# The attention of a fused attention and feed-forward kernel, beside the second product, recast as quadrants of 64 by 64

## The chip, the cores and the metric

The kernel runs on one core of one Trainium2 chip. The metric is the device time of one execution in microseconds (us). TensorE (PE in the profile, its weight loads PEld) multiplies into PSUM; VectorE (DVE), ScalarE (ACT) and GpSimd (POOL) do the rest; SyncE (SP) issues most of the transfers.

## The reference, cut to what matters

```
q_n = q / sqrt(mean(q*q) + 1e-6) * g_q            # k likewise; batch 8, heads 12, seq 448, head_dim 64
attn = softmax((q_n @ k_n.T) / sqrt(64))          # per batch and head, 448 x 448
x = (attn @ v) laid out as (8*448, 12*64)         # 3584 x 768
h = x @ w_in                                      # 768 -> 2048
out = (max(h, 0) ** 2) @ w_out                    # 2048 -> 768
```

All arrays are f32 on the chip.

## The kernel before, in words

The unit of the attention is a *pair*: two heads of one batch entry, 64 dimensions each, so that both fill 128 partitions. There are 8 * 6 = 48 pairs. The feed-forward part works on *spans* of two batch entries, four spans in all. Both products of a span are done by a scheme with seven products of blocks instead of eight (the names A11, S1, S2 and so on); the sums that this scheme needs are made by VectorE and GpSimd.

The order of every engine's work is written out by hand (a manual schedule): each engine executes in the order in which the Python code issues. The program runs as follows.

1. `attention_alone` does the 12 pairs of the first span (i below NAT = 12) while the weights are prepared.
2. For each span: `first_product` (matmuls on L1042), then `second_product` (matmuls into `ps`, L1089). Beside the second product of spans 0, 1 and 2 runs `attention` for the 12 pairs of the next span: both are generators, and the loop takes a share of the second product's matmuls after each `yield` of the attention. The last span's second product runs alone.

The change touches only the 36 pairs of `attention`, thus three stages. One iteration i of it issues, in this order:

- `scores(i, 0)` and `scores(i, 1)` (matmuls L758): keys in chunks of 128 (NF = 3 whole chunks, c = 0 to 2, and a rest of 64 keys, c = 3), all 448 queries as the moving operand. The result has keys on partitions; head h goes to its own PSUM bank, `sc[:, h]`. ScalarE turns both heads of a chunk into `pr` with one Exp (L761). The tiles of `sc` come from a pool of two, so chunks 3 and 2 wait for the Exp of chunks 0 and 1; `pr` goes to one of five places that are used in turn, one of which `fold` of the pair before has just read (L793).
- `values(i - 1)`, which calls `later_values`: the value product of the pair before. Head h fills partitions h*64 to h*64+63 of the bank `pav` (L834). The rest of 64 keys is laid out on 128 partitions as two halves of 224 queries (`sides`), in the tile `half`; its second half goes to another bank, `rest` (L840).
- `spread(i - 1)`: two DMAs on ScalarE's queue (L805) that copy the pair's softmax factors to the partitions of `xT`. They wait for the factors' way through DRAM (L992, on SP's queue).
- `scores(i, 3)` and `scores(i, 2)`, then ScalarE's copy of `rest` out of PSUM (L968), then `norm_by_squares` and `transposes` for later pairs.
- VectorE adds up the exponentials (`add_up`, L782 and L784), does `finish(i - 1)` (L876 adds `rest` to `pav`, L877 multiplies by the factors and writes `xT`), and `fold(i)` (L792 to L799), which makes the factors.

In an iteration's schedule the second product's matmuls come between these steps, mostly after the last scores. Its results leave PSUM through VectorE (L1100 to L1108) or ScalarE (L1098) and are written out by `deliver` (L1077, L1080). In span 0, VectorE makes the second product's sums as well (`combine`, L1003 to L1007).

A matmul of this kernel shows as two records of TensorE, each with its own weight load. The form `64*128` in the profile means 64 rows of contraction and 128 columns of weights; `64*64` is a quadrant of the array.

Of the kernel before, what the change touches and what calls it, by code (L numbers as in the profile page):

```python
# [9 lines left out]
F32 = mybir.dt.float32  # L10
U32 = mybir.dt.uint32
AF = mybir.ActivationFunctionType
ALU = mybir.AluOpType
# [373 lines left out]
def attention_then_ffn_bounded(  # L387
# [35 lines left out]
    nc = tc.nc  # L423

    B, H, S, D = q.shape
    NT, DM = out.shape
    DFF = w_in.shape[1]
    P = 128
# [9 lines left out]
    NF = S // P  # L438
    sides = [slice(m * P // 2, (m + 1) * P // 2) for m in range(2)]
# [15 lines left out]
    ps_o = ctx.enter_context(tc.tile_pool(name="ps_o", bufs=1, space=bass.MemoryType.PSUM))  # L455
# [8 lines left out]
    qk, qkT, ident, mhalf, gains, rstd0, _ = held  # L464
# [189 lines left out]
    vs, probs, pavs, tots, normed, rstds = {}, {}, {}, {}, {}, {0: rstd0}  # L654
    places, halves, rests = [], [], {}
    sums = {"out": [dram.tile([2 * S // 32, 32], F32, name=f"factors{n}") for n in range(2)]}

    def load(i):
        if i < NAT:
            load_q(nc, qk, q, i)  # L660
            load_k(nc, qk, k, i)
            return

        b, h0 = i // NPAIR, 2 * (i % NPAIR)
        for s, src in enumerate((q, k)):
            dst = by_squares(i, 0)[:, s]
            for n in range(4):
                nc.sync.dma_start(dst[n * 32:(n + 1) * 32],
                                  src[b, h0 + n // 2, :, n % 2 * 32:n % 2 * 32 + 32]
                                  .rearrange("(g t) e -> t g e", t=32))  # L670
# [38 lines left out]
    def squares(i):  # L709
        raw, qkn = (by_squares(i, n).rearrange("p s g e -> p (s g e)") for n in range(2))  # L710
        nc.scalar.activation(qkn, raw, AF.Square)
# [19 lines left out]
    def transposes(i):  # L731

        qkn = normed.pop(i)
        for s in range(2):
            nc.vector.transpose(qkT[:, 0, s], qkn[:, s].rearrange("p g e -> p (g e)"))
        nc.scalar.activation(qkT[:, 0, 0], qkT[:, 0, 0], AF.Copy, scale=gains[:, 0:1])
# [11 lines left out]
    def scores(i, c):  # L748


        if i >= NAT:
            sc = ps_s.tile([P, 2, 512], F32, tag="s", name="sc")
            n = S if c < NF else S // 2
            for h in range(2):
                rows = slice(h * D, (h + 1) * D)
                for m in range(S // n):
                    part = slice(0, P) if c < NF else sides[m]
                    nc.tensor.matmul(sc[part, h, 0:n], qkT[rows, 0, 1, c * P:min((c + 1) * P, S)],  # L758
                                     qkT[rows, 0, 0, m * n:(m + 1) * n], start=True, stop=True)
            pr = probs[i, c] = places[(NF * i + c) % len(places)] if c < NF else halves[i % 2]  # L760
            nc.scalar.activation(pr, sc[:, :, 0:n], AF.Exp)  # L761
            return
        at = i % 2
        sc = ps_s.tile([SP, 2, 512], F32, tag="s", name="sc")
        for h in range(2):
            rows = slice(h * D, (h + 1) * D)
            nc.tensor.matmul(sc[:, h, 0:S], qkT[rows, at, 1, c * SP:(c + 1) * SP], qkT[rows, at, 0, :],  # L767
                             start=True, stop=True)
        pr = probs[i, c] = places[(NJ * i + c) % len(places)][:SP]
        for h in range(2):  # L770
            nc.scalar.activation(pr[:, h], sc[:, h, 0:S], AF.Exp, scale=rstds[i][:, 1, 2 * c + h:2 * c + h + 1])
# [4 lines left out]
    def add_up(i, c):  # L776

        acc = acc_of(i)
        if i >= NAT and c == NF:
            for m, rows in enumerate(sides):  # L780
                part = acc[rows, :, m * S // 2:(m + 1) * S // 2]
                nc.vector.tensor_tensor(part, part, probs[i, c][rows], ALU.add)  # L782
            return
        nc.vector.tensor_tensor(acc, probs[i, 0] if c == 1 else acc, probs[i, c], ALU.add)  # L784
# [16 lines left out]
    def spread(i):  # L801

        b, hp = divmod(i, NPAIR)
        for h in range(2):
            nc.scalar.dma_start(xT[h * D:(h + 1) * D, b % 2, hp],  # L805
                                sums["out"][i % 2].rearrange("(h g) t -> h () (g t)", h=2)[h].to_broadcast([D, S]))
# [12 lines left out]
    def values(i, chunks=range(NJ)):  # L819
        if 0 in chunks:  # L820
            pavs[i] = ps_o.tile([P, S], F32, tag="o", name="pav") if i >= NAT or i % 2 == 0 else bank("pav", 1)
        if i >= NAT:
            return later_values(i)
        for c in chunks:
            for h in range(2):
                nc.tensor.matmul(pavs[i][h * D:(h + 1) * D, :], vs[i][:SP, h, c, :], probs[i, c][:, h, :],  # L826
                                 start=(c == 0), stop=(c == NJ - 1))

    def later_values(i):


        for c in range(NF):
            for h in range(2):
                nc.tensor.matmul(pavs[i][h * D:(h + 1) * D, :], vs[i][:, h, c, :], probs[i, c][:, h, :],  # L834
                                 start=(c == 0), stop=False)
        rests[i] = ps_o.tile([P, S], F32, tag="t", name="rest")
        for h in range(2):
            for m, rows in enumerate(sides):
                into = rests[i] if m else pavs[i]
                nc.tensor.matmul(into[h * D:(h + 1) * D, 0:S // 2], vs[i][rows, h, NF, :], probs[i, NF][rows, h, :],  # L840
                                 start=bool(m), stop=True)

    def added(i):

# [12 lines left out]
    def finish(i):  # L857

        b, hp = divmod(i, NPAIR)
        pav, factors = pavs.pop(i), xT[:, b % 2, hp]  # L860
        x = factors
        if i < NAT:


            turned, factors = sums["turned"], sums["factors"]
            few = small.tile([P, S // 32], F32, tag="few", name="few", bufs=1)
            nc.vector.transpose(turned, tots.pop(i))
            nc.vector.reciprocal(few, turned.rearrange("p (g r) -> p g r", r=32)[:, :, 0])
            nc.vector.transpose(factors.rearrange("p (g r) -> p g r", r=32),
                                few.rearrange("p g -> p g ()").to_broadcast([P, S // 32, 32]))  # L870

            x = x.rearrange("d (p j) -> d j p", j=NJ)
            pav, factors = (t.rearrange("d (j p) -> d j p", j=NJ) for t in (pav, factors))
        else:
            half = pav[:, S // 2:]
            nc.vector.tensor_tensor(half, half, rests.pop(i), ALU.add)  # L876
        nc.vector.tensor_tensor(x, pav, factors, ALU.mult)  # L877
        del vs[i]

# [14 lines left out]
    def attention_alone():  # L894


        for i in range(NAT):
# [34 lines left out]
            total_of(i - 1)  # L932
            values(i, (0, 1))
            finish(i - 1)
            yield
            if added(i) == 3:
# [5 lines left out]
        values(i, (2, 3))  # L942
        total_of(i)
        finish(i)
        combine_x(i)

    def attention(first):


        last = first + 2 * NPAIR  # L950
        for i in range(first, last + 1):
            if i < last:
                scores(i, 0)
                scores(i, 1)
            if i + 3 < min(last + 2, B * NPAIR):
                load(i + 3)
            if i == first:
                yield
            if i > first:
                values(i - 1)  # L960
                spread(i - 1)
            if i < last:
                add_up(i, 1)
                scores(i, 3)
                scores(i, 2)
            if i > first:
                rest = halves[(i - 1) % 2].rearrange("p h q -> p (h q)")[:, 0:S // 2]
                nc.scalar.copy(rest, rests[i - 1][:, 0:S // 2])  # L968
                rests[i - 1] = rest
            if i + 2 < last:  # L970
                norm_by_squares(i + 2)
            yield
            if i + 1 < last:
                transposes(i + 1)
            if i < min(last, B * NPAIR - 1):
                load_v(i + 1)
            yield
            if i < last:
                add_up(i, 2)
                add_up(i, 3)  # L980
            if i > first:
                finish(i - 1)
            if i + 3 < last:
                squares(i + 3)
            yield
            if i < last:
                fold(i)
            if i > first:
                combine_x(i - 1)
            yield  # L990
            if i < last:
                nc.sync.dma_start(sums["out"][i % 2], sums["square"][0:2 * S // 32, 1])  # L992
            yield
# [168 lines left out]
    for span in range(NSPAN):  # L1162
# [7 lines left out]
        with tc.tile_pool(name="second_product", bufs=2, reuse_waits="tile") as work:  # L1170
            rest = second_product(work, span)
# [101 lines left out]
```

## Time and profile before

| | |
|---|---|
| three runs | 1391.18, 1392.67 (median), 1393.52 us |
| profiled execution, first to last instruction (span) | 1389.0 us; the median lies 3.7 us above it, and no other time of the profiled execution is given |
| TensorE busy | 1360.9 us, 98% of the span |
| VectorE, GpSimd, ScalarE busy | 60%, 41%, 30% |
| `attention` beside the second product | about 263 to 457, 600 to 787 and 930 to 1115 us |
| scores L758, forms 64\*128 and 64\*64 | 432 and 288 records |
| values L834 (128\*64), rests L840 (64\*64) | 432 and 288 records |
| L876, L877 (VectorE), L968 (ScalarE) | 36 each, 400, 624 and 346 ns |

How to read it: an engine that is busy 98% of the span sets the time nearly everywhere, and the others matter where TensorE waits for them. A record of a matmul overlaps the next, so what one costs is the distance between starts, not its duration.

### The profile page before, as it was taken

The page shows a single profiled execution, that of the slowest core. Times are in us where ns is not written, and L with a number is a line of the kernel's source. Part 1 is how long each engine was busy: PE and PEld are TensorE (multiplying, and loading weights), DVE is VectorE, ACT ScalarE, POOL GpSimd, SP SyncE. Part 2 cuts the span into 40 slices and gives each one's busy share as a digit, 9 for nine tenths or more (in the row PEclk, how much of TensorE's full clock was granted, in tenths as well). Part 3 has the DMA queues.
Part 4 walks back from the last instruction along what each step waited for, and adds up shares of the span by engine and source line. Part 5 has one row for each costly group of instructions (what it writes and reads, how often), then busy time and mean ns, then how long its engine had stood idle before and what let it go on. Part 6 is the DMA issues. An engine that isn't in the chain of part 4 may idle for free.

```text
span 1389.0 us, 15124 instructions
## 1 busy us (share of the span) xinstructions
PE 1360.9 (98%) x4738; PEld 636.1 (46%) x4738; DVE 829.7 (60%) x1470; ACT 418.0 (30%) x657; POOL 572.1 (41%) x397
## 2 busy tenths in 40 slices
PE   8989999999999999999999999999999999999997
PEld 3333455444444455444444455444444445554553
DVE  6889676599987333477877623457888723332111
ACT  7875555422332011233332111233333201110000
POOL 5998878544343022644344122445445302220000
PEclk9999999999999999999999999999999999999999
DMA  8687998544666333344665432345574442333443
GB/s 239 194 231 197 327 387 307 160 107 106 125 134 130 102 87 86 99 116 105 134 144 120 106 99 86 100 104 116 109 148 108 103 103 85 88 91 100 109 112 67
DMA packets 436678, 190.02 MB, mean 137 GB/s; under 512 B 283244, under 2 KB 434540, under 8 KB 436588
## 3 DMA queue, kind: packets, MB, share of 16 engines
q1 hardware_dynamic: 426988, 180.23, 50.2%
q10 hardware_dynamic: 9472, 8.72, 2.4%
q8 instruction: 40, 0.66, 0.2%
q14 instruction: 50, 0.41, 0.1%
q0 software_dynamic: 128, 0.00, 0.0%
HBM read 155.72 MB, written 33.16 MB: 136 GB/s over the span
## 4 chain that ended last, share of the span: by engine, by line
PE 85%; DVE 6%; POOL 3%; issue 2%; DMA 2%; ACT 2%; SPq 1%; ACTq 0%; POOLq 0%
PE ps L1089 33%; PE pd L1042 10%; PE pa L1042 10%; PE pc L1042 10%; PE sc L758 7%; PE pav L834 5%; PE pb L1042 5%; PE sc L767 1%; PE pav L840 1%; PE tot L854 1%; PE pav L826 1%; POOL rstd L702 1%; DMA sw<-w1s 1%; POOL gC L566 1%; DMA factors<-square 1%
## 5 line engine op out<-in xcount | busy, mean ns | idle before, releaser
L1089 PE MATMUL ps<-gT,sw 128*128 128x448 f32 x768 | 299.2, 543 | 0.8 <-POOL gT L1019 0.8
L724 POOL TENSOR_TENSOR half<-half,mhalf 128x28 f32<-128x28 f32 x36 | 173.6, 4822 | 267.6 <-DVE half L723 249.3
L1089 PE MATMUL ps<-gC,sw 128*128 128x448 f32 x576 | 225.5, 543 | 2.9 <-ACT p L1098 1.5
L1019 POOL TENSOR_TENSOR gT<-gT 128x448 f32<-128x448 f32 x96 | 94.9, 990 | 303.7 <-ACT gT L1015 303.7
L1089 PEld LDWEIGHTS ps<-gT,sw 128*128 128x128 f32 x768 | 144.1, 190 | 149.3 <-issue 145.2
L1089 PEld LDWEIGHTS ps<-gC,sw 128*128 128x128 f32 x576 | 107.9, 190 | 115.8 <-issue 108.4
L1042 PE MATMUL pa<-xT,sw 128*128 128x448 f32 x384 | 154.9, 540 | 0.0
L1015 ACT ACTIVATE gT<-gT 128x448 f32<-128x448 f32 x96 | 55.4, 577 | 311.1 <-DVE gT L1057 311.1
L758 PE MATMUL sc<-qkT 64*128 64x448 f32 (+1 forms) x720 | 118.8, 484 | 0.7 <-ACT pr L761 0.4
L761 ACT ACTIVATE pr<-sc 128x896 f32<-128x896 f32 x87 | 77.3, 914 | 133.1 <-DVE quarters L793 62.1
L1042 PEld LDWEIGHTS pa<-xT,sw 128*128 128x128 f32 x384 | 73.0, 190 | 71.6 <-issue 70.5
L1057 DVE TENSOR_TENSOR gT<-z,pd 128x448 f32<-128x448 f32 x32 | 19.8, 620 | 99.7 <-PE pd L1042 99.7
L1042 PE MATMUL pb<-xC,sw 128*128 128x448 f32 x192 | 77.5, 540 | 1.5 <-issue 1.5
L1042 PE MATMUL pc<-xC,sw 128*128 128x448 f32 x192 | 77.5, 540 | 0.6 <-DMA sw<-w1s 0.6
L1042 PE MATMUL pd<-xT,sw 128*128 128x448 f32 x192 | 77.9, 542 | 0.0
L1042 PE MATMUL pd<-xC,sw 128*128 128x448 f32 x192 | 77.5, 540 | 0.1
L1042 PE MATMUL pc<-xT,sw 128*128 128x448 f32 x192 | 77.4, 539 | 0.0
L834 PE MATMUL pav<-pr,vt 128*64 128x448 f32 x348 | 74.2, 548 | 3.2 <-DVE xT L877 3.2
L726 POOL TENSOR_TENSOR qk<-qk,half 128x448 f32<-128x448 f32 x72 | 74.2, 1051 | 2.8
L572 POOL TENSOR_TENSOR gC<-gC 128x384 f32<-128x384 f32 x64 | 73.2, 1161 | 2.5
L758 PEld LDWEIGHTS sc<-qkT 64*128 64x128 f32 (+1 forms) x720 | 46.2, 165 | 54.3 <-issue 42.9
L1049 DVE TENSOR_TENSOR z<-p,pb 128x448 f32<-128x448 f32 x32 | 19.8, 619 | 82.4 <-PE pb L1042 82.4
(132 smaller groups left out, 1757.0 us busy)
## 6 DMA issues: line engine op xcount, KB each, us to landing
sw<-w1s SPq DMA_DIRECT2D x224, 192.0 KB, 2.4
sw<-w2s SPq DMA_DIRECT2D x168, 256.0 KB, 3.3
w1s<-gC SPq DMA_DIRECT2D x8, 1344.0 KB, 7.6
w2s<-gC SPq DMA_DIRECT2D x8, 1344.0 KB, 8.7
out_dram<-osb SPq DMA_DIRECT2D x184, 56.0 KB, 1.9
qk<-in_q_dram SPq DMA_DIRECT2D x144, 56.0 KB, 2.9
qk<-in_k_dram SPq DMA_DIRECT2D x144, 56.0 KB, 2.6
xT<-factors ACTq DMA_DIRECT2D x72, 112.0 KB, 3.4
```

The costliest lines, as they stand in the source:

```text
L572: nc.gpsimd.tensor_tensor(*[blocks_of(n)[:, i] for i in (dst, x, y)], op)
L724: nc.gpsimd.tensor_tensor(half, half, mhalf, ALU.pow)
L726: nc.gpsimd.tensor_tensor(qkn[:, s], raw[:, s], half[:, s * NG:(s + 1) * NG].rearrange("p g -> p g ()").to_broadcast([P, NG, 32]), ALU.mult)
L758: nc.tensor.matmul(sc[part, h, 0:n], qkT[rows, 0, 1, c * P:min((c + 1) * P, S)], qkT[rows, 0, 0, m * n:(m + 1) * n], start=True, stop=True)
L761: nc.scalar.activation(pr, sc[:, :, 0:n], AF.Exp)
L834: nc.tensor.matmul(pavs[i][h * D:(h + 1) * D, :], vs[i][:, h, c, :], probs[i, c][:, h, :], start=(c == 0), stop=False)
L1015: nc.scalar.activation(g, src, AF.Relu)
L1019: nc.gpsimd.tensor_tensor(g, g, g, ALU.mult)
L1042: nc.tensor.matmul(ps, stream[n + i][:, c], rhs[:, c], start=first and c == 0, stop=c == HC - 1, skip_group_check=not first)
L1049: add(z, p1, ps, ALU.add)
L1057: add(g, x, ps, ALU.add)
L1089: nc.tensor.matmul(ps, stream[n][:, c % 4], rhs_of[i][:, c], start=c == 0, stop=c == HF - 1)
```

## The change

All scores of `attention` are issued as quadrants: a chunk of 128 keys becomes two matmuls of 64 keys per head, on the two halves of the output partitions. All value products are issued as quadrants too: a chunk of 128 keys is split into its two halves of partitions, the first accumulating in `pav` and the second in `rest`, both over the full 448 queries. Scores go from 10 to 16 matmuls per pair, values from 10 to 16. Because `rest` now holds a partial sum for all 448 queries, ScalarE copies 448 columns of it where it copied 224, VectorE adds 448 columns where it added 224, and writes the sum to SBUF (into the copy of `rest`), from which the multiplication then reads. The order of all steps, the tiles and their numbers are as before.

```diff
@@ scores
-                for m in range(S // n):
-                    part = slice(0, P) if c < NF else sides[m]
-                    nc.tensor.matmul(sc[part, h, 0:n], qkT[rows, 0, 1, c * P:min((c + 1) * P, S)],
-                                     qkT[rows, 0, 0, m * n:(m + 1) * n], start=True, stop=True)
+                for m, part in enumerate(sides):
+                    keys = slice(c * P + m * D, c * P + (m + 1) * D) if c < NF else slice(NF * P, S)
+                    of = slice(0, S) if c < NF else slice(m * n, (m + 1) * n)
+                    nc.tensor.matmul(sc[part, h, 0:n], qkT[rows, 0, 1, keys], qkT[rows, 0, 0, of], start=True, stop=True)
@@ later_values
-        for c in range(NF):
+        rests[i] = ps_o.tile([P, S], F32, tag="t", name="rest")
+        for c in range(NF + 1):
             for h in range(2):
-                nc.tensor.matmul(pavs[i][h * D:(h + 1) * D, :], vs[i][:, h, c, :], probs[i, c][:, h, :],
-                                 start=(c == 0), stop=False)
-        rests[i] = ps_o.tile([P, S], F32, tag="t", name="rest")
-        for h in range(2):
-            for m, rows in enumerate(sides):
-                into = rests[i] if m else pavs[i]
-                nc.tensor.matmul(into[h * D:(h + 1) * D, 0:S // 2], vs[i][rows, h, NF, :], probs[i, NF][rows, h, :],
-                                 start=bool(m), stop=True)
+                for m, rows in enumerate(sides):
+                    into = (rests[i] if m else pavs[i])[h * D:(h + 1) * D]
+                    into = into if c < NF else into[:, m * S // 2:(m + 1) * S // 2]
+                    nc.tensor.matmul(into, vs[i][rows, h, c, :], probs[i, c][rows, h, :],
+                                     start=(c == 0), stop=(c == NF), skip_group_check=True)
@@ finish
-            half = pav[:, S // 2:]
-            nc.vector.tensor_tensor(half, half, rests.pop(i), ALU.add)
+            rest = rests.pop(i)
+            nc.vector.tensor_tensor(rest, pav, rest, ALU.add)
+            pav = rest
         nc.vector.tensor_tensor(x, pav, factors, ALU.mult)
@@ attention
-                rest = halves[(i - 1) % 2].rearrange("p h q -> p (h q)")[:, 0:S // 2]
-                nc.scalar.copy(rest, rests[i - 1][:, 0:S // 2])
+                rest = halves[(i - 1) % 2].rearrange("p h q -> p (h q)")
+                nc.scalar.copy(rest, rests[i - 1])
```

## The prediction

> **What bounds the kernel now.** I read the page's busy shares first, then the chain of waits, then the timeline of TensorE within one iteration of the attention, then the windows of its stages.
>
> ```profile
> span 1389.0 us, 15124 instructions
> PE 1360.9 (98%) x4738; PEld 636.1 (46%) x4738; DVE 829.7 (60%) x1470; ACT 418.0 (30%) x657; POOL 572.1 (41%) x397
> ...
> PE 85%; DVE 6%; POOL 3%; issue 2%; DMA 2%; ACT 2%; SPq 1%; ACTq 0%; POOLq 0%
> ```
>
> TensorE sets the time nearly everywhere. But its busy time hides gaps between tiling forms; these show in the starts. One iteration (start, length, records):
>
> ```profile
> 408.61 1.78 PE L758 MATMUL sc<-qkT 64*128 64x448 f32 x8
> 410.32 2.48 PE L834 MATMUL pav<-pr,vt 128*64 128x448 f32 x12
> 412.72 0.40 PE L840 MATMUL pav<-half,vt 64*64 64x224 f32 x1
> ...
> 412.96 0.35 PE L840 MATMUL pav<-half,vt 64*64 64x224 f32 x1
> ...
> 413.15 1.51 PE L758 MATMUL sc<-qkT 64*64 64x224 f32 x12
> 414.59 4.78 PE L1089 MATMUL ps<-gC,sw 128*128 128x448 f32 x12
> ```
>
> The x12 at 413.15 holds 8 records of 64\*64 and 4 of 64\*128. The unit comes from the weight loads of the second product, one per record:
>
> ```profile
> 410.31 0.20 PEld L834 LDWEIGHTS pav<-pr,vt 128*64 128x64 f32 x4 [0.65 <-DVE quarters L795]
> 410.75 0.14 PEld L834 LDWEIGHTS pav<-pr,vt 128*64 128x64 f32 x2 [0.23 <-issue]
> 411.12 0.14 PEld L834 LDWEIGHTS pav<-pr,vt 128*64 128x64 f32 x2 [0.23 <-issue]
> ...
> 413.64 0.30 PEld L758 LDWEIGHTS sc<-qkT 64*128 64x128 f32 x4 [0.33 <-issue]
> ...
> 415.45 0.19 PEld L1089 LDWEIGHTS ps<-gC,sw 128*128 128x128 f32 x1 [0.18 <-issue]
> 415.82 0.19 PEld L1089 LDWEIGHTS ps<-gC,sw 128*128 128x128 f32 x1 [0.18 <-issue]
> ```
>
> A record of 448 columns takes 0.3755 us of TensorE, in every form: the pairs of 128\*64 follow each other at the same distance (410.75, 411.12), two abreast. A group of four quadrants of 224 columns takes half of that, 0.188: from the last group of `rest` (412.96) to the first of the scores (413.15) it is 0.19. So four quadrants do run abreast at full rate, and between two groups of the same form nothing is lost, even where tiles and PSUM banks change. The work of the iteration is then 4 pairs (1.502), 6 pairs (2.253), 2 quadrant groups (0.376), 2 groups and 2 pairs (1.127): 5.26 us. It took 414.59 - 408.61 = 5.98. The missing 0.72 us lie at the changes of form: the first record of the new form starts 0.1 us late, and its second load cannot be hidden (0.05 us for 64 columns of weights, 0.1 for 128).
>
> VectorE matters in part of span 0:
>
> ```profile
> 285.50:352.00 66.50, 61.33 (x254) 26.55 (x252) 62.27 (x116) 19.01 (x29) 29.65 (x12) 1.00 0.49 108
> ...
> 657.00:788.00 131.00, 131.00 (x549) 58.19 (x550) 104.22 (x204) 37.74 (x55) 50.54 (x28) 1.00 0.58 128
> ```
>
> In this view of windows (length, then busy PE, PEld, DVE, ACT, POOL) VectorE is busy 94% from 285.5 to 352 and TensorE has 5.2 us of gaps; later it is at 80% and TensorE has none.
>
> **What the Trainium skill says.** *TensorEngine Tiling (Array Packing)*, Tiling Modes, Key Properties: changing the tiling mode, not just the tile, drains the engine, and tiles work independently. The trace agrees with both, at 0.1 us for the drain. The same page, Gotcha 1: PSUM Pressure: different row tiles may not write one PSUM bank at once; that is why the value product needs `pav` and `rest` and a later addition. *SBUF — State Buffer*, Who interferes with whom: a VectorE instruction with two SBUF inputs contends with GpSimd instructions that read SBUF. The trace agrees: L782, two SBUF inputs, takes 1.25 us beside GpSimd's L726, and 0.78 in the mean. The changed L877 becomes such an instruction.
>
> **The change part by part.**
>
> *TensorE, a full iteration.* Records go from 40 matmuls to 64 (12 more f32 matmuls, two records each), but groups of four replace pairs, so the streaming stays 5.26. Remaining: the one load that cannot be hidden after the product, now of 64 columns (412.72 to 412.96 less 0.19: 0.05), and the drain before the product (in the tail of span 1 the last quadrant group starts at 786.55 and the product at 786.85; less 0.19: 0.11). Sum 5.42, against 5.98: **0.56 us less**. Per stage there are 11 such iterations. The stage's first scores give 0.04 (a shorter load, a slightly longer drain), the scores 3 and 2 of the first iteration 0.21 (600.88 to 602.37 is 1.49; new 0.05 + 0.376 + 0.751 + 0.11 = 1.28), the last value product 0.16 (783.90 to 786.85 is 2.95; new 2.79). Per stage 0.41 + 11 x 0.56 = 6.57, three stages **19.7 us**: the ceiling.
>
> *VectorE and ScalarE.* The rows by form:
>
> ```profile
> L876 DVE TENSOR_TENSOR pav<-pav,half 128x224 f32<-128x224 f32 x36 | 14.4, 400 | 13.3 <-ACT half L968 12.3
> L877 DVE TENSOR_TENSOR xT<-pav,xT 128x448 f32<-128x448 f32 x36 | 22.5, 625 | 2.6 <-DMA xT<-factors 0.9 <-DVE pav L876 0.4
> L1106 DVE TENSOR_TENSOR ct<-p,ps 128x448 f32<-128x448 f32 x24 | 14.6, 610 | 57.4 <-PE ps L1089 57.4
> L968 ACT COPY half<-rest 128x224 f32<-128x224 f32 x36 | 12.5, 346 | 35.9 <-PE rest L840 23.7 <-DMA xT<-factors 12.2
> L1098 ACT COPY p<-ps 128x448 f32<-128x448 f32 x12 | 6.4, 537 | 36.9 <-PE ps L1089 36.9
> ```
>
> L876 becomes an addition of PSUM and SBUF into SBUF over 448 columns, as L1106: 610 ns, +0.21. L877 with both inputs in SBUF: 617 to 644 by L1003 and L1004, to 0.89 beside GpSimd (L892); I take +0. L968 becomes a copy of 448, as L1098: +0.19. `pav` is free after L876 instead of L877, 0.4 us earlier, so that wait of `values` relaxes; the bank of `rest` is free after L968, some 5 us before it is wanted. Where VectorE has slack, +0.21 costs nothing; where it is the chain, it counts.
>
> *What of the ceiling is lost.* Three places.
> - Span 0, 285.5 to 367: the chain runs on VectorE until 352.10 (TensorE's L758 waits for the Exp that ended at 352.05). TensorE's gain before it, 0.25 + 0.56 = 0.81, is carried; the five iterations in it gain nothing, and four L876 add 0.84. The next iteration has only 0.17 us between the Exp's end (367.12) and the scores (367.29); with a fifth L876 and TensorE 0.47 us earlier there, it waits again. Net up to there +0.13; after it five iterations and the tail, 5 x 0.56 + 0.16 = 2.96. Span 0: **-2.8**.
> - Span 1: a chain from 637.56 (VectorE's `ct`) through L876, `fold`, SP, the factors' DMA, ScalarE's two DMAs, Exp, L968 and the copy L1098 to TensorE at 656.86. It starts 0.25 + 2 x 0.56 = 1.37 earlier, is 0.21 + 0.19 longer, and swallows one iteration's gain; then 8 x 0.56 + 0.16 = 4.64. **-5.6**.
> - Span 2: the same chain (to 985.10), and after it a wait of 0.27, because the Exp ends at 993.06 and the scores start at 993.33. **-5.3**.
>
> Sum **-13.8 us**. Made against the span that is 1375.2; the median lies 3.7 above the span, which I keep: 1392.67 - 13.8 = **1378.9**.
>
> **Rivals.**
> *VectorE's loop closes in later.* Each iteration has the loop fold, DMA, Exp, `add_up`, `finish`, fold. If with TensorE at 14.6 instead of 15.2 us per iteration it binds in half of the 21 free iterations (4 of 8, 4 of 8, 3 of 5), 11 x 0.56 = 6.2 are lost: 1385.1. For it: 80% busy and L877 open to GpSimd. Against: in most iterations after 660 `finish` ends 3 to 6 us before `values` starts.
> *The ceiling.* If the waits at the chains shift instead of swallowing: 1373.0. Against: VectorE at 94%.
> *Issue becomes the bound, slower.* An iteration hands TensorE 128 records (loads and matmuls) instead of 80. At 5.98 us that is 46.7 ns each; above this the change loses. The price: *TensorE: Matmul & The Clock Gate*, Wait — 56ns, not 53.3ns?, gives about 62 ns per MATMUL when the sequencer decodes; charged to loads as well, 128 x 62 = 7.9 us, +1.95 per iteration, times 33: +64, 1457. For it: the longest run of quadrants before is 32 records. Against: these took 0.62 us, 19 ns each, though they may have been queued ahead.
> *It doesn't do what it says*: wide quadrants go two abreast only. That adds 6 x 0.75 us per iteration, 1392.67 + 33 x 4.5 = 1541; the groups of 224 in four abreast speak against it. I count it with the former.
>
> **How the numbers follow.** About 0.2%, 2.8 us, can be told from no change. Forecast (-11 to -17) 0.60; ceiling (beyond -17) 0.08; VectorE's loop (-3 to -11) 0.17; nothing within 2.8 us 0.04; slower 0.11. Faster 0.85, same 0.04, slower 0.11. The range 1374 to 1387 takes in the forecast's case, most of the loop's case and half of the ceiling's: 0.8. L877's upper bound (+0.26 on the two or three chains) and the drain's spread (0.09 to 0.11) lie inside it.
>
> **What would show it.** Right: forms 64\*128 and 128\*64 are gone from the scores and values of `attention`; from the scores' first start to the product's 5.4 us; four starts of 448-column quadrants within 0.03 us and the next four 0.376 later; L876's successor near 610, L968's near 540. Loss: more idle time of TensorE before 352, waits of scores for the Exp near 367 and 993. Wrong: starts of quadrants 0.75 apart or spread out (issue), or TensorE idle in every iteration behind the Exp or `finish` (loop).

## The result, and the profile after

Against runs of the kernel before on the same chip the changed kernel takes 0.9917 of the time, with an interval of 0.9902 to 0.9932: medians 1380.51 us (four runs, 1379.54 to 1382.71) and 1391.93 us. That is 11.4 us by the medians, 9.5 to 13.6 by the interval; 13.8 were forecast. The profiled execution of the changed kernel took 1382.71 us, with a span of 1380.9 us. It is the slowest of its four runs, and shows 8.1 us less than the span of before; so the traces below show the losses of one of the longer executions. Runs of one kernel differ by several us, in part with the granted clock: of 27 later runs of the kernel before (those beside e1 to e4), the six at 0.993 or 0.994 took 1392.80 to 1394.80 us and the three at 0.999 or 1.000 took 1388.92 to 1390.46, while two runs of the changed kernel at 0.998 still lie 3.2 us apart.

One iteration of the attention on TensorE, from its timeline (start, length, engine, line, operation, records):

```profile
408.38 1.73 PE L759 MATMUL sc<-qkT 64*64 64x448 f32 x16
409.94 0.54 PE L837 MATMUL pav<-pr,vt 64*64 64x448 f32 x2
409.95 0.54 PE L837 MATMUL rest<-pr,vt 64*64 64x448 f32 x2
410.31 0.54 PE L837 MATMUL pav<-pr,vt 64*64 64x448 f32 x2
...
412.19 0.35 PE L837 MATMUL pav<-half,vt 64*64 64x224 f32 x2
...
412.57 1.31 PE L759 MATMUL sc<-qkT 64*64 64x224 f32 x16
413.81 4.78 PE L1087 MATMUL ps<-gC,sw 128*128 128x448 f32 x12
```

Four wide quadrants start within 0.02 us and the next four 0.37 later: four abreast, at the full rate. The iteration takes 413.81 - 408.38 = 5.43 us, where it took 5.98. The weight loads of the same stretch show that only the load after the product stays unhidden:

```profile
408.38 0.21 PEld L759 LDWEIGHTS sc<-qkT 64*64 64x64 f32 x8 [0.65 <-issue]
408.81 0.15 PEld L759 LDWEIGHTS sc<-qkT 64*64 64x64 f32 x4 [0.22 <-issue]
409.19 0.15 PEld L759 LDWEIGHTS sc<-qkT 64*64 64x64 f32 x4 [0.22 <-issue]
409.56 0.14 PEld L837 LDWEIGHTS pav<-pr,vt 64*64 64x64 f32 x2 [0.22 <-DVE quarters L795]
```

From 408.38 to 408.81 is 0.43; then 0.375 each, also from scores (409.19) to values (409.56), where a change of form lay before.

The steps that grew, from the groups by form:

```profile
L875 DVE TENSOR_TENSOR xT<-half,xT 128x448 f32<-128x448 f32 x36 | 23.6, 655 | 7.7 <-DMA xT<-factors 6.5
L873 DVE TENSOR_TENSOR half<-pav,half 128x448 f32<-128x448 f32 x36 | 22.5, 625 | 11.1 <-ACT half L966 10.0
L966 ACT COPY half<-rest 128x448 f32<-128x448 f32 x36 | 19.2, 534 | 33.0 <-PE rest L837 11.2 <-issue 11.1 <-PE ps L1087 10.8
```

L873 is the former L876 (400 ns), L875 the former L877 (625), L966 the former L968 (346). And the two stretches of VectorE's load:

```profile
285.50:352.00 66.50, 59.61 (x338) 25.81 (x336) 62.30 (x113) 18.81 (x28) 28.89 (x12) 1.00 0.50 110
657.00:788.00 131.00, 130.85 (x766) 60.73 (x764) 107.74 (x208) 38.77 (x54) 52.09 (x28) 1.00 0.59 129
```

In the first, TensorE's gaps grew from 5.2 to 6.9 us; in the second it has hardly any. What they are waits for is read from TensorE's waits between 265 and 1115 us (total, times, longest), first of the kernel before:

```profile
PE pav L834 <- DVE xT L877: 3.2, 2, 2.1
PE ps L1089 <- ACT p L1098: 1.5, 2, 1.1
PE ps L1089 <- POOL half L724: 1.4, 1, 1.4
PE sc L758 <- ACT pr L761: 0.4, 2, 0.2
```

and of the changed kernel:

```profile
PE ps L1087 <- DVE p L1106: 4.2, 3, 2.4
PE sc L759 <- ACT pr L761: 3.0, 8, 0.9
PE pav L837 <- DVE half L873: 2.6, 2, 1.8
PE ps L1087 <- ACT p L1096: 2.6, 2, 1.5
PE ps L1087 <- POOL qk L726: 1.7, 1, 1.7
PE sc L759 <- ACT qkT L761: 0.2, 1, 0.2
```

The first line is new. It belongs to the ends of the three stages, once each. The chain of waits at the end of the first stage (start, length, what):

```profile
440.51 3.91 DMA factors<-square
...
444.95 3.24 DMA xT<-factors
...
449.42 0.64 DVE half L873
...
455.40 0.21 DVE square L799
...
455.63 1.28 DMA factors<-square
...
456.93 0.45 ACTq L805
...
457.42 3.79 DMA xT<-factors
...
461.65 0.63 DVE xT L875
...
464.20 0.53 DVE ct L1104
464.73 0.54 DVE p L1106
...
465.31 2.90 PE ps L1087 x7
```

VectorE stands in `finish` of the last pair until the factors have gone to DRAM and back; `ct` and `p`, which clear a bank that TensorE needs, are queued behind it. In the kernel before, the same two steps at the same place (`p` on VectorE, the next matmuls on TensorE) were these:

```profile
462.24 0.61 DVE L1108 TENSOR_TENSOR p<-p,ps 128x448 f32<-128x448 f32 x1
464.77 6.18 PE L1089 MATMUL ps<-gT,sw 128*128 128x448 f32 x16
```

There `p` was done 1.9 us before TensorE wanted the bank. Now TensorE has ended its last value product 2.0 us earlier, and `p` comes 2.4 us later: it waits 2.4 us. That `p` is late goes further back than its place in the queue. Between 381.6 and 465.3 us this chain holds no matmul: it runs through VectorE's `add_up`, `finish` and `fold` and through the DMAs of several pairs, of which the lines show two.

The stages measured in the traces, in us: to the last value product means from the stage's first scores to the first product matmul after the last value product; the rest goes on to the next first product.

| | span 0 | span 1 | span 2 | sum |
|---|---|---|---|---|
| before, to the last value product | 194.31 | 189.37 | 188.64 | 572.32 |
| before, whole stage | 207.20 | 202.25 | 201.53 | 610.98 |
| after, to the last value product | 191.75 | 183.35 | 183.61 | 558.71 |
| after, whole stage | 207.32 | 196.75 | 198.32 | 602.39 |

Up to the last value product the gain is 2.6, 6.0 and 5.0 us, 13.6 in all. The ends then give back 2.7, 0.5 and 1.8, 5.0 in all, and 8.6 are left. In the first stage nothing is.

### The profile page after: what moved, and what is told of

It reads as the page before. It is cut to its first block, busy times and chain, and to the rows that moved or that the text cites. A ratio compares the mean times of both kernels' runs of the same rounds, so it can differ in the third digit from the quotient of the medians.

```text
span 1380.9 us, 16875 instructions
## 1 busy us (share of the span) xinstructions
PE 1345.1 (97%) x5602; PEld 635.8 (46%) x5602; DVE 844.3 (61%) x1470; ACT 425.2 (31%) x657; POOL 576.4 (42%) x397
## 4 chain that ended last, share of the span: by engine, by line
PE 71%; DVE 11%; DMA 6%; POOL 5%; issue 3%; ACT 2%; SPq 1%; ACTq 1%; DVEq 0%; POOLq 0%
PE ps L1087 25%; PE pd L1040 10%; PE pa L1040 10%; PE pc L1040 10%; PE pb L1040 5%; PE sc L759 4%; PE pav L837 3%; DMA factors<-square 2%; DMA xT<-factors 2%; POOL rstd L702 2%; DVE quarters L793 1%; DVE acc L782 1%; DVE acc L784 1%; POOL gC L566 1%; DVE pr L792 1%
## 5 line engine op out<-in xcount | busy, mean ns | idle before, releaser
L759 PE MATMUL sc<-qkT 64*64 64x448 f32 (+1 forms) x1152 | 111.6, 498 | 3.3 <-ACT pr L761 3.0
L726 POOL TENSOR_TENSOR qk<-qk,half 128x448 f32<-128x448 f32 x72 | 76.5, 1083 | 2.8
L837 PE MATMUL pav<-pr,vt 64*64 64x448 f32 x348 | 72.8, 537 | 2.6 <-DVE half L873 2.6
L837 PE MATMUL rest<-pr,vt 64*64 64x448 f32 x348 | 72.8, 537 | 0.0
```

What stands on the lines that cost most here:

```text
L726: nc.gpsimd.tensor_tensor(qkn[:, s], raw[:, s], half[:, s * NG:(s + 1) * NG].rearrange("p g -> p g ()").to_broadcast([P, NG, 32]), ALU.mult)
L759: nc.tensor.matmul(sc[part, h, 0:n], qkT[rows, 0, 1, keys], qkT[rows, 0, 0, of], start=True, stop=True)
L837: nc.tensor.matmul(into, vs[i][rows, h, c, :], probs[i, c][rows, h, :], start=(c == 0), stop=(c == NF), skip_group_check=True)
```

## The experiments

Each was timed in five rounds beside the kernel before. Within the runs of one kernel the times spread by 3 to 7 us; so the stages of the traces are used beside the ratios. A trace is one execution, and what two traces differ by can be more or less than what two medians differ by.

**Scores alone (e1) and values alone (e2).** The first takes only the change of `scores`; the second takes the others and leaves `scores` as before. In short:

```diff
# e1, against before
-                for m in range(S // n):
-                    part = slice(0, P) if c < NF else sides[m]
+                for m, part in enumerate(sides):
...
# e2, against after
-                for m, part in enumerate(sides):
+                for m in range(S // n):
+                    part = slice(0, P) if c < NF else sides[m]
```

> Only the scores are quadrants; values, rest, copy and finish are those of before. Theory (the gain is the drains and unhidden loads at changes of form): of the four changes inside an iteration one goes (scores 3 to scores 2, 0.21 us) and the first load after the product is shorter (0.05), the others stay (scores to values, values to rest). 0.25 us per full iteration, a stage 3.0 us, three stages 9.0 us at most; some is swallowed where VectorE carries the chain in span 0, so 6 to 8 us faster than before, and VectorE and ScalarE unchanged. Rival (the gain comes from the value side: pav is free 0.4 us earlier because the addition reads it alone): within 2 us of before.

> Only the value products are quadrants (with the longer copy and finish); scores are those of before. Theory: the change from values to rest goes, 0.15 us per iteration, 0.16 at a stage's last value product: 1.8 us per stage, 5.4 at most; VectorE's 0.21 and ScalarE's 0.19 take some back, so 1 to 4 us faster than before. The two halves together then give 0.40 us per iteration and not 0.56: the missing 0.15 is the change between scores and values, which only goes when both are quadrants. Rival (value side carries the gain): 8 us or more faster than before.

Scores alone: 0.9946 (0.9934 to 0.9958), 1385.01 against 1392.34 us, 7.3 us. Values alone: 0.9982 (0.9975 to 0.9990), 1389.77 us, 2.6 us. One iteration of e1 on TensorE's timeline:

```profile
409.07 1.74 PE L759 MATMUL sc<-qkT 64*64 64x448 f32 x16
410.74 2.48 PE L834 MATMUL pav<-pr,vt 128*64 128x448 f32 x12
...
414.81 1.39 PE L1089 MATMUL ps<-gC,sw 128*128 128x448 f32 x3
```

and of e2:

```profile
411.10 1.77 PE L758 MATMUL sc<-qkT 64*128 64x448 f32 x8
412.80 0.59 PE L837 MATMUL pav<-pr,vt 64*64 64x448 f32 x1
...
416.93 3.27 PE L1087 MATMUL ps<-gC,sw 128*128 128x448 f32 x8
```

They take 5.74 and 5.83 us, 0.24 and 0.15 less than 5.98, together 0.39; the whole change gave 0.55. In e1 the step from scores to values still takes 1.67 us where the changed kernel needs 1.56. The gain is thus the changes of form, one by one, and the one between scores and values goes only when both sides are quadrants. The earlier release of `pav`, which e2 has and e1 has not, is not what carries it.

**The short finish (e3).**

```diff
-            rest = rests.pop(i)
-            nc.vector.tensor_tensor(rest, pav, rest, ALU.add)
-            pav = rest
+            half = pav[:, S // 2:]
+            nc.vector.tensor_tensor(half, half, rests.pop(i), ALU.add)
...
-                rest = halves[(i - 1) % 2].rearrange("p h q -> p (h q)")
-                nc.scalar.copy(rest, rests[i - 1])
+                rest = halves[(i - 1) % 2].rearrange("p h q -> p (h q)")[:, 0:S // 2]
+                nc.scalar.copy(rest, rests[i - 1][:, 0:S // 2])
```

> The changed kernel, but ScalarE copies and VectorE adds only 224 columns of rest, as before (this leaves out the second bank's partial sums of half the queries). TensorE's work is that of the changed kernel. Theory (VectorE's and ScalarE's longer steps lie on the chain in span 0, in one chain of spans 1 and 2, and at each stage's end): 2 to 4 us faster than the changed kernel, so 13 to 15 us faster than before. Rival (these steps are hidden everywhere, and what was lost of the ceiling was lost to waits that a faster TensorE meets anyway): within 1 us of the changed kernel.

0.9897 (0.9884 to 0.9910), 1377.81 us: 14.5 us less than before by the medians, and 2.7 below the changed kernel's 1380.51. Its stages are 203.84, 195.81 and 197.34 us, 3.5, 0.9 and 1.0 less than those of the changed kernel. The longer copy and addition do lie on the chain, most of all in span 0. Up to the last value product they cost 0.8, 0.4 and 0.5 us, about as much as the forecast put on them (0.21 us five times in span 0, 0.4 once in the others). The ends are 2.7, 0.5 and 0.5 us shorter: of the 5.0 us that the ends gave back, 3.7 go with the short steps.

**The additions ahead of the last finish (e4).** In a stage's last iteration one unit of the second product, the one that issues `ct` and `p`, comes ahead of `finish`:

```diff
-                    while done < min(total, total * (u + 1) // (10 * NPAIR + 1)):
+                    while done < min(total, total * (u + 1) // (10 * NPAIR + 1)) + (u > 10 * NPAIR):
```

> The changed kernel, but in a stage's last iteration the second product's two additions (ct and p, L1104 and L1106) are issued to VectorE ahead of the last pair's finish, instead of behind it; TensorE's order is the same. Theory (at each stage's end VectorE stands in finish, which waits for the factors' DMA, and TensorE waits for the PSUM bank that p would free: 2.6, 0.4 and 1.7 us in the trace): those three waits go, about 4.7 us faster than the changed kernel, 15 to 17 us faster than before. Rival (the next wait takes their place, the following product needs xT from that same finish): within 1 us of the changed kernel.

VectorE's timeline at the end of the first stage:

```profile
456.66 0.62 DVE L1104 TENSOR_TENSOR ct<-y,ps 128x448 f32<-128x448 f32 x1 [1.44 <-PE ps L1087]
457.20 0.61 DVE L1106 TENSOR_TENSOR p<-p,ps 128x448 f32<-128x448 f32 x1
459.35 0.62 DVE L873 TENSOR_TENSOR half<-pav,half 128x448 f32<-128x448 f32 x1 [1.54 <-ACT half L966]
```

The two additions now run while VectorE would have stood idle, and TensorE's wait for them is gone from its list of waits. The stages are 204.61, 196.17 and 196.47 us, 5.1 less than the changed kernel's in sum; no later wait took the place. By the clock it is less plain: 0.9911 (0.9896 to 0.9926), median 1378.38 us, with two of six runs near 1382. That is 14.0 us less than before and 2.1 less than the changed kernel, where 15 to 17 and 4.7 were expected. By time alone it cannot be told from the changed kernel; what the traces show is that the wait goes.

**Light sums in span 0, on both kernels (e5, e6).**

```diff
-        g11, g12 = gT[:, f, 0:S], gT[:, f, S:2 * S]
...
+        w = S // 14 if f in few else S
+        g11, g12 = gT[:, f, 0:w], gT[:, f, S:S + w]
...
-                    combine(f, (j // 4,))
+                    combine(f, (j // 4,), range(HF))
```

> The kernel before, but VectorE makes the second product's sums of span 0 (L1003 to L1007) over 32 of 448 columns only (the rest of these sums is left out); all else is as before. Partner of e6: their difference is what the change gives where VectorE is not full in span 0. Theory (VectorE carries the chain there): TensorE's gaps between 285 and 352 us go, the first attention stage falls from 207.2 to about 202 us, as long as the two others; about 5 us faster than before. Rival (the gaps there come from the factors' DMA or GpSimd): the stage stays above 205.

> The changed kernel with the same narrowed sums in span 0 as e5 (32 of 448 columns). Theory: the first stage, which gained nothing by the change (207.2 and 207.3 us in the traces), now gains as stage two did (5.5 us): 196 to 198 us, and the kernel is 9 to 12 us faster than the changed kernel and 13 to 15 us faster than e5. Rival (the stage's gain is lost to something other than VectorE's sums): it gains under 2 us against e5's stage.

e5: 0.9967 (0.9954 to 0.9981), 1388.24 us; e6: 0.9869 (0.9850 to 0.9888), 1373.99 us. The windows of the same stretch of span 0 (length, then busy PE, PEld, DVE, ACT, POOL), first e5, then e6, whose stage begins 3.4 us later:

```profile
285.50:352.00 66.50, 65.25 (x269) 29.05 (x268) 56.82 (x133) 21.74 (x33) 31.17 (x13) 1.00 0.54 119
```

```profile
289.00:355.00 66.00, 64.13 (x366) 29.37 (x365) 57.52 (x132) 21.83 (x32) 30.75 (x13) 1.00 0.56 120
```

With VectorE at 85 to 87% in place of 94%, TensorE's gaps in it fall to 1.3 and 1.9 us, and the first stage is 202.36 us without and 197.04 us with quadrants. The stage that gained nothing by the change gains 5.3 us once VectorE has room, as its neighbour of span 1 does (5.5). This was the theory's number. The wait at this stage's end is gone in e6 too, though `ct` and `p` still stand behind `finish`: the lateness of `p` there came from VectorE's load. By the medians e6 is 14.3 us faster than e5, as expected, but e5 is 3.7 faster than before (about 5 expected) and e6 6.5 faster than the changed kernel (9 to 12 expected; its stages are 11.2 less in sum).

**Spread later (e7), and the copy on VectorE instead (e8).** Both on top of e4.

```diff
# e7
                 values(i - 1)
-                spread(i - 1)
...
                 nc.scalar.copy(rest, rests[i - 1])
                 rests[i - 1] = rest
+                spread(i - 1)
# e8
-                nc.scalar.copy(p1s[m], ps)
+                (nc.vector.tensor_copy if 0 < span < NSPAN - 1 else nc.scalar.copy)(p1s[m], ps)
```

> e4 (additions ahead of the last finish), and spread's two DMAs stand on ScalarE's queue behind the Exps of scores 3 and 2 and the copy of rest, instead of ahead of them; nothing else. Theory (ScalarE stands in spread until the factors have come, and the copy L1096 behind it holds TensorE at 651 and 974 us in e4's trace, 1.3 and 1.6 us): those two waits go and the Exps come earlier, 3 to 5 us faster than e4. Rival (the factors now come later, finish waits for them, pav comes free later and values wait): no faster than e4, with VectorE's L875 waiting for the DMA in most iterations.

> e4, and in spans 1 and 2 the copy of the first product A11 out of PSUM (L1096) goes to VectorE, six copies of about 0.6 us. Theory as in e7 (the two waits come from ScalarE's queue order): they go without touching spread, 2 to 3 us faster than e4. Rival (VectorE is as late at that point): the waits stay, now on VectorE, within 1 us of e4.

e7: 0.9850 (0.9836 to 0.9865), 1371.12 us, 20.8 us less than before and 9.4 less than the changed kernel by their medians. Of TensorE's waits between 265 and 1115 us for another engine these are left, all in span 0:

```profile
PE sc L759 <- ACT pr L761: 2.7, 6, 0.9
PE pav L837 <- DVE half L873: 2.0, 2, 1.8
```

Its stages are 201.95, 194.40 and 194.72 us. It gained more than was expected of it (3 to 5 us on e4): 7.3 us by the medians, 6.2 by the stages. e8 missed its 2 to 3 us on e4, and shows that it is not enough to take the one copy out of ScalarE's queue: 0.9898 (0.9882 to 0.9914), 1377.79 us, 0.6 less than e4, stages 597.4 us in sum against e4's 597.3. The wait for `p` went from its list; in its place scores wait for the Exp (4.0 us in place of 2.9) and values for `finish` (3.4 in place of 2.6). The Exps too stood behind the DMAs, and e8 left them there; that this is why e8 gained nothing was not shown by a run of its own.

**The two reorderings without quadrants (e9, e11).** e9 is the kernel before with `spread` moved as in e7; e11 adds e4's edit.

> The kernel before, with spread's DMAs moved as in e7 and nothing else. Theory (spread ahead of the Exps costs the kernel before only the three gaps that its trace shows there, 1.6, 1.3 and 0.5 us; the changed kernel pays more for it because TensorE meets it sooner): 2 to 4 us faster than before, so that the change itself, measured between e9 and e7, is worth 16 to 18 us less the tail's part, nearer to its ceiling of 19.7. Rival (moving spread is worth the same 6 to 7 us in any kernel): 6 us or more faster than before.

> The kernel before with both reorderings of e7 (the additions ahead of the last finish, and spread behind the Exps and the copy); the partner of e7 without the quadrants. Theory (e9 gained little because three new gaps of 0.9 to 1.2 us at the stages' ends ate it; the additions ahead of the last finish take those away): 3 to 5 us faster than before, and the quadrants between this kernel and e7 are worth 15 to 18 us. Rival (moving spread is worth nothing without quadrants, whatever the tail): within 1.5 us of before.

e9 missed: 0.9993 (0.9982 to 1.0004), 1391.44 us, nothing that can be told. Its trace shows why: up to the last value products its stages gain 4.4 us on the kernel before, and the ends give 3.3 back, because TensorE now waits there for `p`. At the first:

```profile
455.82 0.04 ACT half L967
...
456.39 3.32 DMA xT<-factors
...
462.33 0.53 DVE ct L1106
462.86 0.54 DVE p L1108
...
463.45 2.90 PE ps L1089 x7
```

It is the same queue as in the changed kernel, but the edit itself makes `finish` late here: the last pair's DMA now starts only behind ScalarE's last copy (L967). With the additions ahead of the finish as well (e11) it is 0.9977 (0.9970 to 0.9985), 1388.44 us, 3.5 us faster than before. Beside e7, which differs from e11 by the quadrants alone, 1388.44 - 1371.12 = 17.3 us (each was timed on its own chip beside the kernel before, whose median was 1391.90 both times; by the stages it is 15.4): with both reorderings the quadrants are worth most of the ceiling of 19.7.

**Values as before in the first five pairs (e10).** On e7, with the value products, copy and `finish` of those pairs in the old form (`narrow(i)` is true for them).

```diff
+        if narrow(i):
+            ...
+                    nc.tensor.matmul(pavs[i][h * D:(h + 1) * D, :], vs[i][:, h, c, :], probs[i, c][:, h, :],
+                                     start=(c == 0), stop=False)
```

> e7, but the first five pairs of the first stage, where VectorE is full with the second product's sums, have their value products, copy and finish in the form of before (the scores are quadrants). Theory (TensorE waits there anyway, and VectorE has 0.2 us less per pair): the first stage falls from 201.9 us by about 1 us, 0.5 to 2 us faster than e7. Rival (the lost change of forms, 0.3 us per pair, costs more than VectorE's 0.2): equal to or up to 1.5 us slower than e7.

0.9868 (0.9849 to 0.9887), 1372.95 us; the first stage is 201.20 us against e7's 201.95. The stage moved as expected, but the time, 1.8 us above e7's by the medians, cannot be told from it. e7, the simpler, is the best version here.

## Why the prediction was right, point by point

- *The bound and the mechanism*: right. The changes of form were the lost time; an iteration takes 5.43 us (5.42 in the sum), and e1 and e2 split it as the counted transitions do.
- *Four quadrants abreast, and issue*: right. The 128 records of an iteration took 5.43 us, 42 ns each where the rival of the issue rate put 62, and four wide quadrants start together every 0.375 us; that rival and the one of two abreast are out. That both halves of the keys could not share one PSUM bank no run tried; this rests on the page that the prediction names.
- *The steps on VectorE and ScalarE*: L873 took 625 ns (610 taken), L966 534 (537 taken), L875 655 where the old form took 625 (no difference taken). The Trainium skill's *SBUF — State Buffer*, Who interferes with whom, would have such an instruction with two SBUF inputs meet GpSimd. The trace agrees: the three long ones, 0.95 to 1.05 us, stand beside GpSimd's L726; at 0.03 us in the mean it matters little here.
- *What VectorE swallows in span 0*: right. TensorE was to be 0.13 us later after those iterations and was 0.35 later (its product at 369.12, and at 368.25 before, from the stages' starts at 264.11 and 263.59); up to the last value product the stage gained 2.6 (2.8 in the sum). e5 and e6 show the cause.
- *The chain in spans 1 and 2*: right in size: up to the last value product 6.0 and 5.0 us, for 5.6 and 5.3. The three together are 13.6, for 13.8.
- *The step that failed* is the tail. The sum gave each stage's end a gain of 0.16 us and no wait, since the kernel before showed none there. But VectorE already stood idle there for ScalarE's copy (12.3 us at L876, in three waits), with `ct` and `p` queued behind, and `p` was done only 1.9, 1.3 and 2.1 us before TensorE wanted its bank. TensorE then came to the three ends 2.0, 5.4 and 9.9 us earlier, and `p` in the first 2.4 us later, in the others only 3.7 and 6.0 us earlier. So it waits: 5.0 us in the traces. The forecast had asked where a faster TensorE meets the chains that stop it already, not where it meets those that just fail to. With that term the sum is 13.8 - 5.0 = 8.8, and the spans' difference is 8.1.
- *The rival of VectorE's loop* has a part in it. In the iterations after 660 hardly any gap came; but the chain that makes `p` late at the end of the first stage runs through that loop, and with VectorE's sums narrowed (e6) the wait there is gone.
- *The number*: 1380.51 us against 1378.9 is nearer than the sum deserved, and that is in part luck. In the trace the forgotten term is over a third of the forecast; by the medians only 2.4 us are missing, and e4, which takes the waits away, is only 2.1 us faster. The ends of a usual execution may thus cost less than those of the profiled one; this was not shown.

## What to carry to other kernels

Where small matmuls of several tiling forms follow each other, count the changes of form by the distances between starts, and see whether all can take the one form that the smallest needs; here that took 1.6 times the matmuls (32 per pair for 20) for the same streaming time. Then list what the bounding engine nearly waited for, not only what it waited for: a step that stands in a queue behind a DMA's latency, idle and harmless, is the next wait. Putting work whose input is there ahead of work that waits for a transfer gave 9.4 us on the changed kernel (e7) and 3.5 on the kernel before (e11). Half of it can give nothing: `spread` moved alone (e9) made the last pair's DMA late.

## What the runs showed of the hardware that was not expected

- At all five changes of form of the iteration of before that the prediction shows, the cost was the same two parts: 0.09 to 0.11 us before the first record and an unhidden second load of 0.05 us (64 columns of weights) or 0.1 us (128). It did not matter whether the rows or the columns of the tiling changed.
- VectorE's small copies of 32x28 (L795) take 0.17 us, but 0.84 beside GpSimd's subtraction L890, and this stands in the chain at the first stage's end; a fivefold time for the least of its steps. In the kernel before all three together took 0.57 us at that place, so it is 0.7 of the 2.4 us by which `p` was late:

```profile
453.09 1.13 POOL L890 TENSOR_TENSOR xT<-xT 128x448 f32<-128x448 f32 x1
```

```profile
453.41 0.84 DVE quarters L795
```
